# Head 0's operands from the pair's rows on chip, half the warm-up products, and the next pair's cluster products behind the transposes

## The chip, the cores and the metric

One core of a Trainium2 chip runs the whole program in one launch. The metric is device time in microseconds, of the kernel before and of the changed one on the same inputs; the median of several runs counts.

## The reference

Three layers follow each other on float32 data, with batch 2, 8 heads, 768 positions and head width 64.

```python
q_n, k_n, c_n = (x / (norm(x) + 1e-06) for x in (q, k, centroids))   # 16 centroids a head
q_assign = argmax(q_n @ c_n.T); k_assign = argmax(k_n @ c_n.T)
scores = where(q_assign[:, None] == k_assign[None, :], q @ k.T / 8, -1e9)
attn = softmax(scores) @ v
u = x + (relu(x.T @ w_tok1) @ w_tok2).T;   x = u + relu(u @ w_ch1) @ w_ch2
theta = x @ w_theta;  y = w_tok_r @ (x * cos(theta)) + w_tok_i @ (x * sin(theta))
out = (x + y) + relu((x + y) @ w_ch)
```

The change touches the first layer alone, the attention in which a query sees only the keys of its own cluster.

## The kernel before, in words

**Precision.** Every float32 operand is cut into a rounded high part and the remainder (`split_sb` for data in SBUF, `split_ps` for data in PSUM), so that products of parts add up to nearly full precision.

**Attention.** Heads come in pairs. `load_pair` loads the rows of a pair's q and k, 64 partitions a head, and `split_pair` cuts them on GpSimd. `masks` multiplies them with the centroids (the cluster products, tile `sim`, 4 products for the first pair and 12 for the others), turns them over on VectorE (`sT`), finds the largest of 16 (`mx`, `eq`, `eqT`), takes the first of equals by a triangular product (`pp`, `oh`) and writes the one-hot rows scaled (`m`). It is a generator that stops at each `yield`; the main loop takes two steps of it a unit. `place` copies 16 rows of `m` by DMA below the remainder rows in the tiles `q2` and `k2`, so that the second product of a score, `k2` by `q2`, adds the remainder and the mask at once. `prep` fills a head's four operand tiles by DMAs from the pair's parts; `prep_first`, used for heads 0 and 1, loads the head's rows from HBM instead, each twice, into both halves of a tile, and cuts them there.

A unit is 256 queries of a head. `scores` makes two tiles of 128 queries by 768 keys (4 products each, L354 and L355, into one of two PSUM buffers), takes the negated maximum (L359, `nm`) on VectorE and the exp (L361, `e`) on ScalarE. `turn` transposes the exp tiles on TensorE (L376) and cuts them, by ScalarE and VectorE (kind A) or by a ScalarE copy and two GpSimd operations (kind C, the third of each unit). `values` multiplies them with v (L399). Names end in batch, head, unit and tile: `s002` is the third score tile of head 0, `m02` the mask of pair 2.

**Order.** The program is written unit by unit; a scheduler then places each instruction on its engine's queue by its own timeline, in the order of writing where several are ready. `issue_after` keeps what is written inside it behind a named instruction. Engines and the DMA queue of SyncE (SP) work through their queues in order. SP issues nearly every load: rows of pairs, the copies of `prep` and `place`, and from unit 2 on, every four units, 512 columns of the weights w1 and w2 (`load_w`, L94 to L112), which ScalarE (L100, L101), VectorE (L103, L104) and GpSimd (L107) decode.

**Warm-ups.** `warm_up` issues products of a zero tile: `WARM` = 17 at the start, 4 behind the transposed centroids, 20 behind the first cluster products, 18 behind the first two score tiles.

**The start.** L475 loads pair 0's rows, L476 and L477 run its masks, L478 calls `prep_first` for head 0 and L480 for head 1; then `place` and `place_centroids` (clears `csth` and `cstl` on GpSimd, fills them on VectorE at L179). The upper halves of `q2` and `k2` are cleared on GpSimd at L205. In the first masks the rows go into head 0's tiles directly (L249 to L259).

The main loop, cut to the steps the change moves:

```python
for n in range(len(units) + SKEW):
    es[n] = scores(b, h, u, ops[b, h])
    for _ in range(PACE):
        next(gen, None)                     # masks of the next pair
    prs[n - 1] = turn(*units[n - 1], es.pop(n - 1))
    values(b, h, u, prs.pop(n - SKEW), ops[b, h][4])
```

Behind attention come two blocks of matrix products over all positions, which the change leaves as they are.

Of the kernel before, what the change touches and what calls it, by code (L numbers as in the profile page):

```python
# [9 lines left out]
F32 = mybir.dt.float32  # L10
# [8 lines left out]
P = 128  # L19
# [17 lines left out]
PACE = 2  # L37
# [7 lines left out]
SKEW = 2  # L45
WARM = (17, 4, 20, 18)


@with_exitstack
def tile_model(ctx: ExitStack, tc: tile.TileContext, qT, kT, v, cent, w1, w2, wc1, wc2, wth, wri, wch, out):  # L50
# [22 lines left out]
    def split_sb(h, l, x, rnd, sub):  # L73

        if rnd == "p":
            nc.gpsimd.tensor_scalar(out=h, in0=x, scalar1=1.0, scalar2=0.0, op0=ALU.mult, op1=ALU.add)
        elif rnd == "v":
            nc.vector.tensor_copy(out=h, in_=x)
        else:
            nc.scalar.activation(out=h, in_=x, func=AF.Copy)  # L80
        e = nc.gpsimd if sub == "p" else nc.vector
        e.tensor_tensor(out=l, in0=x, in1=h.bitcast(F32), op=ALU.subtract)

# [39 lines left out]
    with ExitStack() as actx:  # L123
# [45 lines left out]
        for j in range(2):  # L169
            r, n = slice(64 * j, 64 * j + 64), slice(96 + CL * j, 96 + CL * j + CL)  # L170
            nc.vector.tensor_copy(out=cst[r, n], in_=cps[r, CL * j : CL * j + CL])

# [31 lines left out]
        k2 = [ap.tile([P, S], F32R, name=f"k2_{i}") for i in range(2)]  # L204
        for t in q2 + k2:  # L205
            nc.gpsimd.memset(t[64:128, :].bitcast(F32), 0.0)

        def masks(b, pr):
# [27 lines left out]
            eqT = mp.tile([P, NH], BF16, tag="eq", bufs=2, name=f"eqT{b}{pr}")  # L236
            turned = nc.vector.transpose(out=eqT, in_=eq)
            marks.setdefault("eqT", turned)
            yield
# [5 lines left out]
            if first:  # L245
                for a in range(2):
                    n = slice(a * NH, a * NH + NH)
                    r = 32 * a
                    nc.vector.tensor_copy(out=q2[0][64 : 64 + CL, n], in_=oh[r : r + CL, :])  # L249
                    r = 64 + 32 * a  # L250
                    if a == 0:
                        nc.scalar.activation(  # L252
                            out=k2[0][64 : 64 + CL, n], in_=oh[r : r + CL, :], func=AF.Copy, scale=BIG, bias=-BIG
                        )
                    else:
                        nc.vector.tensor_scalar(
                            out=k2[0][64 : 64 + CL, n], in0=oh[r : r + CL, :], scalar1=BIG, scalar2=-BIG,
                            op0=ALU.mult, op1=ALU.add,
                        )  # L259
            yield  # L260
# [6 lines left out]
        def prep_first(b, h):  # L267
# [14 lines left out]
            nc.gpsimd.tensor_tensor(out=k1[64:128, :], in0=kr[64:128, :], in1=k1[64:128, :].bitcast(F32), op=ALU.subtract)  # L282
            return qh, q2[i], k1, k2[i], load_v(b, h)

        one = dict(scalar1=1.0, scalar2=0.0, op0=ALU.mult, op1=ALU.add)
# [18 lines left out]
        def split_pair(b, pr, ts):  # L304

            parts = []
            for x, f, k in zip(ts, (scale, 1.0), "qk"):
                hi, lo = (ap.tile([P, S], F32R, tag="hl", bufs=HL, name=f"{k}{j}{b}{pr}") for j in "hl")
                if f != 1.0:
                    nc.gpsimd.tensor_scalar(out=x, in0=x, scalar1=f, scalar2=0.0, op0=ALU.mult, op1=ALU.add)  # L310
                split_sb(hi, lo, x, "p", "p")
                parts += [hi, lo]
# [31 lines left out]
        def scores(b, h, u, ops):  # L344
# [3 lines left out]
            for j in range(2):  # L348
# [9 lines left out]
                nm = ap.tile([P, 1], F32, tag="nm", bufs=4, name=f"nm{b}{h}{qt}")  # L358
                nc.vector.tensor_reduce(out=nm, in_=ps[:, :, :NH], axis=AX.XY, op=ALU.max, negate=True)  # L359
                e = ap.tile([P, S], F32, tag="e", bufs=4, name=f"e{b}{h}{qt}")  # L360
# [7 lines left out]
        def turn(b, h, u, es):  # L368

            pr = []  # L370
            for j in range(NT // 2):
                ps = ps_t.tile([P, 2, 256], F32, tag="t", name=f"t{b}{h}{u}{j}")
                for i in range(2):
                    for a in range(2):
                        kt = 2 * j + a
                        nc.tensor.transpose(ps[:, a, i * P : i * P + P], es[i][:, kt * P : kt * P + P], ident)  # L376
                ph = ap.tile([P, 2, 256], F32R, tag="ph", bufs=6, name=f"ph{b}{h}{u}{j}")
                pl = ap.tile([P, 2, 256], F32R, tag="pl", bufs=6, name=f"pl{b}{h}{u}{j}")
                kind = KINDS[3 * u + j]
                if kind in "BC":  # L380
# [94 lines left out]
        raws = load_pair(0, 0)  # L475
        for _ in masks(0, 0):  # L476
            pass  # L477
        ops = {heads[0]: prep_first(*heads[0])}  # L478
        with tc.issue_after(marks["eqT"].ins):
            ops[heads[1]] = prep_first(*heads[1])  # L480
        place(1, ms[0, 0])
        place_centroids()
        gen = iter(())
# [4 lines left out]
        for n in range(len(units) + SKEW):  # L488
            if n < len(units):
# [4 lines left out]
                es[n] = scores(b, h, u, ops[b, h])  # L494
                if n == 0:
                    for w, k in zip(WARM[1:], ("cps", "sim", "scores")):
                        with tc.issue_after(marks[k].ins):
                            warm_up(w)
# [5 lines left out]
                if p1 < len(heads) // 2:  # L504
# [3 lines left out]
                    if n % 6 == PAIR_AT[1]:  # L508
                        split_pair(*pr, raws)
                    if n % 6 == PAIR_AT[2]:  # L510
                        gen = masks(*pr)
            for _ in range(PACE):
                next(gen, None)
            if n == 42:
                mctx.close()
            if 0 <= n - 1 < len(units):
                prs[n - 1] = turn(*units[n - 1], es.pop(n - 1))
            if 0 <= n - SKEW:
                b, h, u = units[n - SKEW]
# [257 lines left out]
```

## Time and profile before

| | |
|---|---|
| time, median of 3 runs | 690.68 us (689.6 to 693.99) |
| the profiled execution | 691.88 us, its span 690.2 us |
| mean granted TensorE clock | 0.988 |
| TensorE busy | 659.0 us, 95% |
| VectorE, ScalarE, GpSimd busy | 436.5, 372.8, 387.2 us |

The span runs from the first to the last instruction; the time holds the launch's ends too. A busy TensorE is one with products in its pipeline, at whichever clock. A clock of 1.00 is 2.4 GHz, 0.50 is 1.2 GHz. Idle time of an engine that nobody waits for costs nothing, so the chain of work that ended last and the idle times with their releasers say more than shares do.

### The profile page before, as it was taken

How to read it: one execution, taken by the hardware profiler on the slowest of the kernel's cores; microseconds unless marked ns; L12 is line 12 of the kernel's file. 1: busy time of each engine (PE TensorE's matmuls, PEld its weight loads, DVE VectorE, ACT ScalarE, POOL GpSimd, SP SyncE). 2: the span in 40 equal slices, each digit the busy share in tenths (PEclk: the TensorE clock that was granted, in tenths of full speed). 3: DMA queues.
4: the chain of work that ended last, by engine and by line, in shares of the span. 5: the costliest groups of instructions: out<-in, count | busy, mean ns of one | idle time of the engine just before them, and what ended most of it. 6: DMA issues, size and time to landing. Idle time of an engine off the chain costs nothing.

```text
span 690.2 us, 10585 instructions
## 1 busy us (share of the span) xinstructions
PE 659.0 (95%) x3772; PEld 578.1 (84%) x3772; DVE 436.5 (63%) x710; ACT 372.8 (54%) x722; POOL 387.2 (56%) x376
## 2 busy tenths in 40 slices
PE   7899989889999999999999999999999999999998
PEld 4798878788998999897888888888888777888886
DVE  6788788978888968558664533445657876523122
ACT  3687768676968777526553431135668684320000
POOL 8977779685866664437884640331456797432000
PEclk9899989999999999999999999999999999999999
DMA  9545645476344330003442321030021233320001
GB/s 264 142 108 165 173 106 146 104 222 180 81 93 92 86 76 1 1 1 123 134 142 92 122 91 33 9 114 2 0 62 61 88 95 93 123 61 32 16 30 47
DMA packets 24533, 62.27 MB, mean 90 GB/s; under 512 B 4320, under 2 KB 7584, under 8 KB 24480
## 3 DMA queue, kind: packets, MB, share of 16 engines
q1 hardware_dynamic: 24480, 61.59, 32.1%
q8 instruction: 30, 0.49, 0.3%
q14 instruction: 23, 0.19, 0.1%
HBM read 40.44 MB, written 3.15 MB: 63 GB/s over the span
## 4 chain that ended last, share of the span: by engine, by line
PE 74%; DVE 6%; DMA 6%; ACT 5%; POOL 4%; issue 3%; SPq 2%; ACTq 0%; POOLq 0%; DVEq 0%
PE o L399 7%; PE t L376 6%; PE r L118 5%; PE r L119 5%; PE r L120 5%; PE c L118 5%; PE c L119 5%; PE c L120 5%; PE y L120 4%; PE y L118 4%; PE y L119 4%; PE s L354 3%; PE s L355 3%; DMA w_raw<-w 3%; ACT e L361 2%
## 5 line engine op out<-in xcount | busy, mean ns | idle before, releaser
L359 DVE TENSOR_REDUCE nm<-s 128x1 f32<-128x768 f32 x96 | 90.9, 949 | 20.9 <-PE s L355 20.3
L361 ACT ACTIVATE e<-s,nm 128x768 f32<-128x768 f32 x96 | 86.9, 906 | 23.0 <-DVE nm L359 12.7
L376 PE MATMUL t<-ident,e 128*128 128x128 f32 x576 | 80.6, 275 | 5.9 <-DVE pl L86 4.7
L399 PE MATMUL o<-ph,vs 128*128 128x256 f32 x288 | 77.3, 298 | 3.0 <-DVE xt L406 3.0
L354 PE MATMUL s<-k,qh 128*128 128x384 f32 x192 | 70.7, 369 | 9.0 <-ACT e L361 6.8
L376 PEld LDWEIGHTS t<-ident,e 128*128 128x128 f32 x576 | 67.8, 142 | 10.5 <-DVE pl L86 4.3
L399 PE MATMUL o<-pl,vs 128*128 128x256 f32 x288 | 74.8, 291 | 0.3 <-POOL pl L387 0.3
L86 DVE TENSOR_TENSOR pl<-t,ph 128x512 fp32r<-128x512 f32 x96 | 62.9, 678 | 6.5 <-ACT ph L85 4.8
L355 PE MATMUL s<-k,q 128*128 128x384 f32 x192 | 65.7, 343 | 1.3 <-ACT k L252 1.3
L85 ACT ACTIVATE ph<-t 128x512 fp32r<-128x512 f32 x96 | 54.9, 598 | 17.6 <-PE t L376 14.8
L387 POOL TENSOR_TENSOR pl<-pr,ph 128x512 fp32r<-128x512 f32 x48 | 62.9, 1310 | 2.0
L386 POOL TENSOR_SCALAR ph<-pr 128x512 fp32r<-128x512 f32 x48 | 30.3, 632 | 57.6 <-ACT pr L382 51.4
L399 PEld LDWEIGHTS o<-ph,vs 128*128 128x128 f32 x288 | 56.1, 195 | 4.0 <-DVE xt L406 3.7
L118 PE MATMUL r<-ul,c_h 128*128 128x512 f32 x144 | 56.7, 394 | 0.0
L399 PEld LDWEIGHTS o<-pl,vs 128*128 128x128 f32 x288 | 56.1, 195 | 0.5 <-POOL pl L387 0.5
L118 PE MATMUL y<-zl,k_h 128*128 128x512 f32 x144 | 56.1, 390 | 0.0
L120 PE MATMUL y<-zh,k_h 128*128 128x512 f32 x144 | 56.1, 389 | 0.0
L119 PE MATMUL y<-zh,k_l 128*128 128x512 f32 x144 | 56.0, 389 | 0.0
L119 PE MATMUL r<-uh,c_l 128*128 128x512 f32 x144 | 56.0, 389 | 0.0
L120 PE MATMUL r<-uh,c_h 128*128 128x512 f32 x144 | 55.9, 389 | 0.0
L120 PE MATMUL c<-c_h,rh 128*128 128x512 f32 x144 | 55.9, 389 | 0.0
L119 PE MATMUL c<-c_h,rl 128*128 128x512 f32 x144 | 55.8, 389 | 0.0
(201 smaller groups left out, 1686.3 us busy)
## 6 DMA issues: line engine op xcount, KB each, us to landing
c_raw<-wc SPq DMA_DIRECT2D x24, 512.0 KB, 3.4
k_raw<-wri SPq DMA_DIRECT2D x18, 512.0 KB, 3.6
qh<-qh SPq DMA_DIRECT2D x28, 192.0 KB, 3.0
k<-kh SPq DMA_DIRECT2D x28, 192.0 KB, 3.7
ql<-qT SPq DMA_DIRECT2D x8, 384.0 KB, 4.2
kl<-kT SPq DMA_DIRECT2D x8, 384.0 KB, 4.4
vr<-v SPq DMA_DIRECT2D x16, 192.0 KB, 3.3
w_raw<-w SPq DMA_DIRECT2D x6, 512.0 KB, 4.0
```

The lines of the kernel that those rows point to most:

```text
L85: nc.scalar.activation(out=h, in_=ps, func=AF.Copy)
L86: nc.vector.tensor_tensor(out=l, in0=ps, in1=h.bitcast(F32), op=ALU.subtract)
L118: nc.tensor.matmul(ps, ah, bl, start=first and i == 0, stop=False)
L119: nc.tensor.matmul(ps, al, bh, start=False, stop=False)
L120: nc.tensor.matmul(ps, ah, bh, start=False, stop=last and i == n - 1)
L354: nc.tensor.matmul(ps[:, half, :NH], qh[:, c], k1[:, n], start=True, stop=False)
L355: last = nc.tensor.matmul(ps[:, half, :NH], ql[:, c], kk[:, n], start=False, stop=True)
L359: nc.vector.tensor_reduce(out=nm, in_=ps[:, :, :NH], axis=AX.XY, op=ALU.max, negate=True)
L361: nc.scalar.activation(out=e.rearrange("p (a n) -> p a n", a=2), in_=ps[:, :, :NH], func=AF.Exp, bias=nm, accum_out=sums[b, h // 2][:, qt, ...
L376: nc.tensor.transpose(ps[:, a, i * P : i * P + P], es[i][:, kt * P : kt * P + P], ident)
L387: nc.gpsimd.tensor_tensor(out=pl, in0=raw, in1=ph.bitcast(F32), op=ALU.subtract)
L399: nc.tensor.matmul(ps[:, :256], vs[:, kt, :], p[:, kt % 2, :], start=n == 0 and k == 0, stop=n == NT - 1 and k == 1,)
```

## The change

Head 0's four operand tiles are made from the pair's rows, which are on chip for the cluster products anyway (`prep_pair_first`): two ScalarE operations, one GpSimd and two VectorE operations, and one more on ScalarE, each of 64 partitions. The subtraction of k, on GpSimd before, is VectorE's. The clears of `q2` and `k2` are split, head 1's behind the copy of k. Head 1's `prep_first` is issued behind the first unit's maxima. The scaled k rows of the first mask are both ScalarE's. The third tiles of units 0 and 1 of head 0 are cut by ScalarE and VectorE in place of GpSimd. The next pair's mask steps are written behind `turn` in place of ahead of it, and for three units are kept behind a transpose. The cutting of later pairs is kept behind the one before. The fourth group of warm-ups has 9 products.

```diff
-WARM = (17, 4, 20, 18)
+WARM = (17, 4, 20, 9)
...
-        for t in q2 + k2:
-            nc.gpsimd.memset(t[64:128, :].bitcast(F32), 0.0)
+        def clear(i):
+            for t in (q2[i], k2[i]):
+                nc.gpsimd.memset(t[64:128, :].bitcast(F32), 0.0)
+        clear(0)
...
-                    if a == 0:
-                        nc.scalar.activation(
-                            out=k2[0][64 : 64 + CL, n], in_=oh[r : r + CL, :], func=AF.Copy, scale=BIG, bias=-BIG
-                        )
-                    else:
-                        nc.vector.tensor_scalar(
...
+                    nc.scalar.activation(
+                        out=k2[0][64 : 64 + CL, n], in_=oh[r : r + CL, :], func=AF.Copy, scale=BIG, bias=-BIG
+                    )
...
+        def prep_pair_first(ts):
+            q, k = (t[0:64, :] for t in ts)
+            qh = ap.tile([P, S], F32R, tag="qh", bufs=2, name="qh00")
+            k1 = ap.tile([P, S], F32R, tag="k1", bufs=2, name="k100")
+            marks["k1"] = nc.gpsimd.tensor_scalar(out=k1[0:64, :], in0=k, **one)
+            nc.scalar.activation(out=qh[0:64, :], in_=q, func=AF.Copy, scale=scale)
+            nc.vector.tensor_tensor(out=k1[64:128, :], in0=k, in1=k1[0:64, :].bitcast(F32), op=ALU.subtract)
+            nc.scalar.activation(out=qh[64:128, :], in_=q, func=AF.Copy, scale=scale)
+            nc.vector.scalar_tensor_tensor(
+                out=q2[0][0:64, :], in0=q, scalar=scale, in1=qh[0:64, :].bitcast(F32), op0=ALU.mult, op1=ALU.subtract
+            )
+            nc.scalar.activation(out=k2[0][0:64, :], in_=k, func=AF.Copy)
+            return qh, q2[0], k1, k2[0]
...
-                kind = KINDS[3 * u + j]
+                kind = "A" if (b, h) == (0, 0) and u < 2 else KINDS[3 * u + j]
...
-        for _ in masks(0, 0):
+        first = masks(0, 0)
+        next(first)
+        vs00 = load_v(0, 0)
+        with tc.issue_after(marks["cst"].ins):
+            ops = {heads[0]: prep_pair_first(raws) + (vs00,)}
+        for _ in first:
             pass
-        ops = {heads[0]: prep_first(*heads[0])}
-        with tc.issue_after(marks["eqT"].ins):
-            ops[heads[1]] = prep_first(*heads[1])
+        with tc.issue_after(marks["k1"].ins):
+            clear(1)
+            place_centroids()
         place(1, ms[0, 0])
-        place_centroids()
...
                 if n == 0:
+                    with tc.issue_after(marks["max"].ins):
+                        ops[heads[1]] = prep_first(*heads[1])
...
-                        split_pair(*pr, raws)
+                        with tc.issue_after(marks["cut"].ins) if p1 > 1 else nullcontext():
+                            split_pair(*pr, raws)
...
-            for _ in range(PACE):
-                next(gen, None)
             if n == 42:
                 mctx.close()
             if 0 <= n - 1 < len(units):
                 prs[n - 1] = turn(*units[n - 1], es.pop(n - 1))
+            with tc.issue_after((marks["turn"] if n else marks["scores"]).ins) if n < 3 else nullcontext():
+                for _ in range(PACE):
+                    next(gen, None)
```

At the start VectorE's queue stands so before, from the centroids' copy to the end of the first cluster search. `cst`, `csth` and `cstl` are placed centroids, `q_0` is head 0's `q2`:

```order
L171 COPY cst<-cps 64x16 x2
L86 TENSOR_TENSOR ctl<-cps,cth 128x128
L179 CAST csth<-cth 64x4x16 x2
L179 CAST cstl<-ctl 64x4x16 x2
L279 SCALAR_TENSOR_TENSOR q_0_155<-qr_190,qh_196 64x768
L224 STREAM_TRANSPOSE sT_172<-sim_167 128x384
```

And so in the changed kernel:

```order
L171 COPY cst<-cps 64x16 x2
L291 SCALAR_TENSOR_TENSOR q_0_155<-ql_161,qh_177 64x768
L289 TENSOR_TENSOR k_178<-kl_163,k_178 64x768
L86 TENSOR_TENSOR ctl<-cps,cth 128x128
L179 CAST csth<-cth 64x4x16 x2
L228 STREAM_TRANSPOSE sT_170<-sim_165 128x384
L179 CAST cstl<-ctl 64x4x16 x2
```

Head 0's two remainders have come ahead of the placed centroids, and `sT` between the two pairs of casts.

On the same engine around units 10 and 11, where pair 2's mask `m02` is written, before (`nm` maxima, `pl` remainders of exp tiles, `xt` output rows):

```order
L244 SCALAR_TENSOR_TENSOR oh02_957<-pp02_958,eqT02_875 128x384
L406 TENSOR_TENSOR xt02_669<-o020_906,tmp020_919 64x256
L359 TENSOR_REDUCE nm032_1013<-s032_1008 128x1
L86 TENSOR_TENSOR pl0220_969<-t0220_963,ph0220_968 128x512
L262 TENSOR_SCALAR m02_961<-oh02_957,mab_150 128x384
L86 TENSOR_TENSOR pl0221_978<-t0221_972,ph0221_977 128x512
L359 TENSOR_REDUCE nm033_1022<-s033_1017 128x1
```

And in the changed kernel:

```order
L418 TENSOR_TENSOR xt02_651<-o020_888,tmp020_901 64x256
L371 TENSOR_REDUCE nm032_995<-s032_990 128x1
L86 TENSOR_TENSOR pl0220_945<-t0220_939,ph0220_944 128x512
L371 TENSOR_REDUCE nm033_1004<-s033_999 128x1
L86 TENSOR_TENSOR pl0221_954<-t0221_948,ph0221_953 128x512
L247 SCALAR_TENSOR_TENSOR oh02_968<-pp02_969,eqT02_886 128x384
L371 TENSOR_REDUCE nm034_1087<-s034_1082 128x1
L259 TENSOR_SCALAR m02_972<-oh02_968,mab_150 128x384
```

`m02` has moved behind `nm033`, `pl0221` and `nm034`.

SP's queue around the placing of that mask, before, and the load of the weights `w1_2`:

```order
L290 DMA vr05_1195<-v 128x384
L322 DMA q2_0_155<-m02_961 16x384 x2
L322 DMA k2_0_157<-m02_961 16x384 x2
L94 DMA w1_2_raw_1088<-w1 128x1024
L322 DMA q2_1_156<-m02_961 16x384
```

And in the changed kernel:

```order
L302 DMA vr05_1177<-v 128x384
L349 DMA qh05_1165<-qh02_691 64x768
L334 DMA q2_0_155<-m02_972 16x384 x2
L334 DMA k2_0_157<-m02_972 16x384 x2
L94 DMA w1_2_raw_1070<-w1 128x1024
```

A load of `qh05` has come ahead of the placing.

## Rows read from the trace of the kernel before

**Rows 1.** Busy time by stretch (us, busy us of each engine, granted clock, DMA share, GB/s).

```profile
14.30:21.20 6.90, 6.02 (x25) 4.50 (x26) 4.65 (x7) 3.68 (x6) 6.74 (x8) 0.51 0.56 190
30.00:40.00 10.00, 9.53 (x70) 8.80 (x71) 9.89 (x17) 8.86 (x20) 7.31 (x7) 1.00 0.58 135
...
89.50:96.40 6.90, 5.77 (x24) 5.70 (x25) 5.24 (x9) 2.97 (x6) 4.18 (x4) 0.51 0.88 182
```

**Rows 2.** Chain of work that ended last, first 60 us (start us, us, what).

```profile
4.16 5.17 DMA kr<-kT
...
10.99 2.09 POOL k L282
...
13.74 0.19 PE pp L243
...
13.96 0.57 DVE oh L244
...
17.50 3.86 PE wps L140 x18
21.36 0.17 PE s L354
```

**Rows 3.** Timeline of ScalarE, start (start us, us, what, [idle before <-releaser]).

```profile
18.23 0.90 ACT L361 ACTIVATE e<-s,nm 128x768 f32<-128x768 f32 x1 [1.80 <-DVE nm L359]
```

**Rows 4.** Tile kl, first load, issued at 1.80 us.

```profile
DMA to landing us min/median/max: 4.5/4.5/4.5
```

**Rows 5.** Timeline of VectorE, start.

```profile
5.76 0.36 DVE L171 COPY cst<-cps 64x16 f32<-64x16 f32 x2 [0.48 <-PE cps L162]
...
6.73 0.49 DVE L179 CAST csth<-cth 64x64 fp32r<-64x64 f32 x2
...
8.79 0.95 DVE L279 SCALAR_TENSOR_TENSOR q<-qr,qh 64x768 fp32r<-64x768 f32 x1 [1.16 <-ACT qh L276]
9.66 0.57 DVE L224 STREAM_TRANSPOSE sT<-sim 128x384 f32<-128x384 f32 x1
...
11.44 0.58 DVE L237 STREAM_TRANSPOSE eqT<-eq 128x384 bf16<-128x384 bf16 x1
...
25.23 0.96 DVE L359 TENSOR_REDUCE nm<-s 128x1 f32<-128x768 f32 x1 [1.30 <-PE s L355]
```

**Rows 6.** Timeline of GpSimd, start.

```profile
1.91 0.73 POOL L206 MEMSET q<- 64x768 f32 x1
...
5.25 0.85 POOL L176 MEMSET csth<- 128x896 f32 x1
...
9.50 0.93 POOL L277 TENSOR_SCALAR k<-kr 128x768 fp32r<-128x768 f32 x1 [2.32 <-DMA kr<-kT]
...
17.20 1.80 POOL L282 TENSOR_TENSOR k<-kr,k 64x768 fp32r<-64x768 f32 x1
```

**Rows 7.** Timeline of VectorE, 117 to 127 us.

```profile
123.08 1.68 DVE L104 SCALAR_TENSOR_TENSOR w_f<-w_f,w_raw 128x512 uint32<-128x512 uint32 x1
```

**Rows 8.** Timeline of GpSimd, the same stretch.

```profile
122.96 1.26 POOL L387 TENSOR_TENSOR pl<-pr,ph 128x512 fp32r<-128x512 f32 x1
```

**Rows 9.** Timeline of VectorE, around m02.

```profile
69.18 0.67 DVE L86 TENSOR_TENSOR pl<-t,ph 128x512 fp32r<-128x512 f32 x1
69.78 0.94 DVE L359 TENSOR_REDUCE nm<-s 128x1 f32<-128x768 f32 x1
```

**Rows 10.** Timeline of SP's queue, around m02's placing.

```profile
69.28 1.18 SPq L322 DMA_DIRECT2D q<-m  x2
...
80.70 0.64 SPq L94 DMA_DIRECT2D w_raw<-w  x1
```

**Rows 11.** Timeline of ScalarE, 52 to 88 us.

```profile
54.12 0.67 ACT L100 ACTIVATE w_f<-w_raw 128x512 f32<-128x512 f32 x1 [1.24 <-DMA w_raw<-w]
...
78.37 0.60 ACT L382 ACTIVATE pr<-t 128x512 f32<-128x512 f32 x1
```

**Rows 12.** Who waited for whom, 30 to 315 us (us in total, times, longest).

```profile
ACT w_f L100 <- DMA w_raw<-w: 5.9, 5, 2.1
```

More of the change, by code (lines that the diff above doesn't have):

```diff
@@ L1 @@
 import math
-from contextlib import ExitStack
+from contextlib import ExitStack, nullcontext
 import concourse.bass as bass
@@ L81, in split_sb @@
         e = nc.gpsimd if sub == "p" else nc.vector
-        e.tensor_tensor(out=l, in0=x, in1=h.bitcast(F32), op=ALU.subtract)
+        return e.tensor_tensor(out=l, in0=x, in1=h.bitcast(F32), op=ALU.subtract)
     def split_ps(h, l, ps):
@@ L170, in tile_model @@
             r, n = slice(64 * j, 64 * j + 64), slice(96 + CL * j, 96 + CL * j + CL)
-            nc.vector.tensor_copy(out=cst[r, n], in_=cps[r, CL * j : CL * j + CL])
+            marks["cst"] = nc.vector.tensor_copy(out=cst[r, n], in_=cps[r, CL * j : CL * j + CL])
         def place_centroids():
@@ L236, in masks @@
             eqT = mp.tile([P, NH], BF16, tag="eq", bufs=2, name=f"eqT{b}{pr}")
-            turned = nc.vector.transpose(out=eqT, in_=eq)
-            marks.setdefault("eqT", turned)
+            nc.vector.transpose(out=eqT, in_=eq)
             yield
@@ L250, in masks @@
                     r = 64 + 32 * a
-                    if a == 0:
-                        nc.scalar.activation(
-                            out=k2[0][64 : 64 + CL, n], in_=oh[r : r + CL, :], func=AF.Copy, scale=BIG, bias=-BIG
-                        )
-                    else:
-                        nc.vector.tensor_scalar(
-                            out=k2[0][64 : 64 + CL, n], in0=oh[r : r + CL, :], scalar1=BIG, scalar2=-BIG,
-                            op0=ALU.mult, op1=ALU.add,
-                        )
+                    nc.scalar.activation(
+                        out=k2[0][64 : 64 + CL, n], in_=oh[r : r + CL, :], func=AF.Copy, scale=BIG, bias=-BIG
+                    )
             yield
@@ L310, in split_pair @@
                     nc.gpsimd.tensor_scalar(out=x, in0=x, scalar1=f, scalar2=0.0, op0=ALU.mult, op1=ALU.add)
-                split_sb(hi, lo, x, "p", "p")
+                marks["cut"] = split_sb(hi, lo, x, "p", "p")
                 parts += [hi, lo]
@@ L358, in scores @@
                 nm = ap.tile([P, 1], F32, tag="nm", bufs=4, name=f"nm{b}{h}{qt}")
-                nc.vector.tensor_reduce(out=nm, in_=ps[:, :, :NH], axis=AX.XY, op=ALU.max, negate=True)
+                marks["max"] = nc.vector.tensor_reduce(out=nm, in_=ps[:, :, :NH], axis=AX.XY, op=ALU.max, negate=True)
                 e = ap.tile([P, S], F32, tag="e", bufs=4, name=f"e{b}{h}{qt}")
@@ L375, in turn @@
                         kt = 2 * j + a
-                        nc.tensor.transpose(ps[:, a, i * P : i * P + P], es[i][:, kt * P : kt * P + P], ident)
+                        marks["turn"] = nc.tensor.transpose(ps[:, a, i * P : i * P + P], es[i][:, kt * P : kt * P + P], ident)
                 ph = ap.tile([P, 2, 256], F32R, tag="ph", bufs=6, name=f"ph{b}{h}{u}{j}")
                 pl = ap.tile([P, 2, 256], F32R, tag="pl", bufs=6, name=f"pl{b}{h}{u}{j}")
-                kind = KINDS[3 * u + j]
+                kind = "A" if (b, h) == (0, 0) and u < 2 else KINDS[3 * u + j]
                 if kind in "BC":
```

## Prediction, made without a run of the changed kernel

> **What bounds the kernel now.** I read busy time by stretch, the chain of work that ended last, each engine's timeline over the first 26 us, and then who waits for whom in the middle of attention. Between 30 and 40 us TensorE is busy 9.53 of 10 us [rows 1], and the page's slices show nine tenths or more behind attention, which ends near 311 us. What can be won lies in the first 25 us and in the stalls of attention.
>
> At the start the chain is a line of waits [rows 2]. The second copy of head 0's k from HBM is issued at 4.16 and takes 5.17 us; GpSimd rounds it and subtracts until 13.08; TensorE has stood at that wait and gives pp late; VectorE makes oh from 13.96, and the products that lacked its rows end at 17.50. Then 18 warm-up products hold TensorE until 21.36, though the exp that frees a score buffer ended at 18.23 + 0.90 = 19.13 [rows 3]. So a load, a GpSimd subtraction and warm-ups longer than what they cover stand in a row.
>
> The granted clock from 14.3 to 21.2 us is 0.51 [rows 1], the lower of the two levels, 1.2 GHz; TensorE had stood idle ahead of it, at the wait for k. A warm-up costs 3.86/18 = 0.214 us there.
>
> **The change part by part.** The sum is made against the profiled execution's own 691.88 us (span 690.2 and 1.7 around it). The median of the runs shown is 690.68, 1.2 lower, and the gain is taken off that.
>
> *Operands of head 0 from the pair's rows.* Four loads and head 0's own copies go. What is late next? The pair's k rows land at 1.80 + 4.5 = 6.3 [rows 4]; q, issued ahead of it, feeds ScalarE, which has nothing to do then. VectorE, free at 5.76 + 0.36 = 6.12, makes the q remainder until 7.07 (0.95) [rows 5]. GpSimd copies k in 0.93 [rows 6]; as this lies beside a two-input operation of VectorE I add 0.29, by which the subtraction L282 was longer at 10.99 (2.09) [rows 2], where VectorE ran such operations too, than at 17.20 (1.80) [rows 6]: until 7.5. The subtraction of k on VectorE has no row: it lies between the 0.95 of the q remainder and GpSimd's 2.09. I take 1.0, next to the row that has its engine and size. It ends at 8.5, not 13.08.
>
> Most of that is lost again, because VectorE's order changes too: the casts into csth now stand ahead of sT, and they wait for GpSimd's clearing of csth, which comes behind the copy of k and two other clears: 7.5 + 2 x 0.73 + 0.85 = 9.8 [rows 6]. With 0.49 for the casts sT starts at 10.3. Before, sT to the end of eqT took 9.66 to 12.02, 2.36 us [rows 5]; the casts into cstl now stand in between (0.49 at most): 13.15, against 12.02. But pp then follows at once, since TensorE no longer stands at k, and the clears and casts are done. From pp's start to oh's 0.22 us passed (13.74 to 13.96 [rows 2]); with as much as 0.35, for pp's own start too, oh starts at 13.5, not 13.96: **0.46 us**.
>
> The collision can be harder than 0.29. L104 on VectorE took 1.68 from 123.08, beside a GpSimd subtraction that ran from 122.96 to 124.22 [rows 7, 8]: it ended 0.5 us after that one, as if it had first waited it out. Then the copy of k would start at 7.07 and end at 8.0, and the 0.46 is gone. The Trainium skill's page "SBUF — State Buffer" (section "The single rule") says that of a VectorE instruction with two SBUF inputs and a GpSimd instruction that reads SBUF the second one blocks until the first is done. By it the sum would be 0.5 smaller; the row of 123.08 agrees, the 0.29 of L282 is too little for it.
>
> *A second block of mask rows goes from VectorE to ScalarE.* One operation each way, beside TensorE's first products. I count nothing; without that cover it is one operation of about half a microsecond.
>
> *Nine warm-ups less.* 9 x 0.214 = **1.93 us** [rows 2]. The products end at 17.50 - 0.46 = 17.04, nine warm-ups at 18.97. The exp before s002 starts at 18.23 - 0.46 = 17.77 and ends at 18.67 [rows 3], so the warm-ups still end last, by 0.3 us.
>
> Sum for s002: 2.39 us earlier. But it runs at the low clock: its first product at 21.36 shows 0.17 [rows 2], at half clock 0.34, four of them cost 0.7 more. **1.7 us** is left. Bounds: 0.5 less with the harder collision; if the clock did not fall this time, the six products before (6 x 0.17) would end 1.0 earlier too and the exp would decide, s002 at 17.7, 3.7 gained.
>
> *Work moved between engines.* Two tiles of exp values leave GpSimd for VectorE, 2 x 0.67 = 1.34 us [rows 9]. VectorE is busy 9.89 of 10 us from 30 to 40 [rows 1], so this isn't free; its cover is the wait of 1.30 before the row at 25.23 [rows 5], which goes as the scores now follow closely. Head 1's q remainder moves behind the first two maxima, into VectorE's next wait for scores. Cost taken 0, up to 1.3 if that cover fails.
>
> *Cluster products behind the transposes.* The order is rearranged through all of attention. In pair 2, m02 now stands behind nm033, pl0221 and nm034: 0.94 + 0.67 + 0.94 = 2.55 us later [rows 9]. SP issues in order: the placing of m02 from 69.28, then the weights w1_2 [rows 10]. A load of qh05 (an issue is 0.6 [rows 10]) stands ahead of both now: 3.1 later. ScalarE reaches w1_2 later by e035 and two copies, 0.90 + 2 x 0.60 = 2.1 [rows 3, 11], so its wait there grows by **1.0**. w2_0 was issued at 80.70, 14 issues behind 69.28, 0.82 each; now 15, from a start 2.55 later: 3.35, against 2.2 on ScalarE (three copies and a shorter one): **1.15** more. w1_1, however, is issued where it was, behind s015, and ScalarE reaches it behind e023 and three copies, 2.7 later: the wait of **1.24** [rows 11] goes. Together +0.9 on ScalarE, of which TensorE sees a part. All w loads cost ScalarE 5.9 us in 5 waits [rows 12]. From below: these all go. From above: the masks of the next two pairs are later alike, +3.3 in all. I take 0, next to the sum of the three.
>
> Forecast: 690.68 - 1.7 = **689.0 us**, its own range 685.5 to 692.
>
> **The rivals.**
>
> *A, slower: the late masks.* w1_2, w2_0 and the two w2 loads behind them wait longer by about 1 us each (3.3 in all with w1_1's gain), all of it reaches TensorE, and one more stretch falls to half clock as 89.5 to 96.4 did (6.9 us at 0.51 [rows 1], 3.4 us lost): 689.0 + 6.7 = 695.7. It decides as soon as these weights land over 2 us after ScalarE reaches them. For it: 5 of the 6 loads already come late. Against it: the same order puts transposes and value products between the halves of s040, which gives placing time.
>
> *B, much faster: the new order loses the stalls.* Half of the 5.9 us reaches TensorE (2.9) and goes, and the half-clock stretch with it (3.4): 689.0 - 6.3 = 682.7. For it: w1_1, and transposes that start right behind s002. Against it: w1_2 and w2_0.
>
> *C, the clock stays low at the start.* Before, warm-ups filled most of the low stretch; now real work does. If the clock comes back one such stretch later, 6.9 us at half speed cost 3.4: 692.4. Against it: from s002 on TensorE has scores, transposes and cluster products in a row.
>
> *D, the start gives the warm-ups only.* With the copy of k blocked the 0.46 goes: 689.5. It is the case where the change doesn't do what it says, the clears being late where k was.
>
> **How the numbers follow.** Forecast 0.43, B 0.20, A 0.14, D 0.12, C 0.11. About 1%, 6.9 us, is what a measurement of this kernel can tell from no change (three runs before span 689.6 to 693.99). Faster by more means below 683.8: most of B, 0.16, and 0.02 of the forecast's tail. Slower means above 697.6: nearly half of A, 0.06, and 0.01 of C. The rest is 0.75. The range goes from B's time to A's, 682.7 to 695.7; the outer halves of both are left out.
>
> **What would show it.** Right: the csth casts wait for GpSimd and sT starts near 10.3; oh near 13.5; nine warm-ups end near 19; in the middle no wait before w1_1's L100, and some 2 us before w1_2's and w2_0's. D: oh at 13.9 or later. C: a clock of 0.5 granted beyond 22 us. A or B: ScalarE's waits for w loads well above or below 5.9 us, and more or fewer half-clock stretches behind 80 us. I am wrong if s002 comes less than 1 us earlier, or if the time moves by over 6 us.

## The result and the profile after

The changed kernel takes 698.21 us (median of 9 runs, 694.02 to 699.14), the kernel before 691.15 beside it (9 runs, 689.6 to 693.99). The ratio is 1.0086, its 95% interval 1.0061 to 1.0111: about 6 us slower. The prediction was 689.0, its range 682.7 to 695.7.

The profiled execution took 699.14 us, span 697.4, against 691.88 and 690.2. It is the longest of the nine runs. The granted clock of these two executions is as low on the mean, 0.987 against 0.988, so the 7 us between them are not the clock's. From the page, the span and the busy time of the engines after:

```profile
span 697.4 us, 10544 instructions
...
PE 659.6 (95%) x3763; PEld 576.8 (83%) x3763; DVE 442.7 (63%) x712; ACT 374.4 (54%) x724; POOL 382.8 (55%) x371
```

TensorE stands idle for 697.4 - 659.6 = 37.8 us; before it was 690.2 - 659.0 = 31.2. Nearly all of the loss is idle time of TensorE, and it does not arise at the start: the maxima of head 0 come 0.3 us earlier to 1.5 later than before, those of head 6 come 1.0 to 3.3 earlier, those of head 9 come 3.7 to 6.8 later. Head 6's lead is not the new start's merit: by then the kernel before has had its stretch of half clock from 89.5 to 96.4 [rows 1], and the changed kernel's comes only at 133.8. The same view as [rows 12], who waited for whom from 30 to 315 us (us in total, times, longest), after:

```profile
PE s L366 <- ACT e L373: 10.7, 12, 2.0
...
ACT w_f L100 <- DMA w_raw<-w: 8.7, 4, 3.6
...
PE o L411 <- DVE xt L418: 6.0, 6, 2.6
...
ACT c_raw L101 <- DMA c_raw<-wc: 2.3, 1, 2.3
...
ACT c_f L100 <- DMA c_raw<-wc: 1.6, 1, 1.6
```

And of the kernel before, beside the row of [rows 12]:

```profile
PE s L354 <- ACT e L361: 5.5, 7, 1.7
PE t L376 <- DVE pl L86: 4.7, 5, 2.4
PE o L399 <- DVE xt L406: 3.0, 2, 2.6
...
ACT c_raw L101 <- DMA c_raw<-wc: 2.2, 1, 2.2
```

ScalarE waits 12.6 us for loads instead of 8.1; TensorE's wait for transposed tiles' remainders (`pl`) shrinks, but its waits for the exp and for the output rows `xt` double. The timelines show one behind the other. ScalarE's timeline after, the weight casts that answer to [rows 11]:

```profile
56.48 0.69 ACT L100 ACTIVATE w_f<-w_raw 128x512 f32<-128x512 f32 x1 [0.99 <-DMA w_raw<-w]
...
81.43 0.65 ACT L100 ACTIVATE w_f<-w_raw 128x512 f32<-128x512 f32 x1 [3.65 <-DMA w_raw<-w]
...
151.99 0.66 ACT L100 ACTIVATE w_f<-w_raw 128x512 f32<-128x512 f32 x1 [2.34 <-DMA w_raw<-w]
...
161.26 0.67 ACT L100 ACTIVATE c_f<-c_raw 128x512 f32<-128x512 f32 x1 [1.61 <-DMA c_raw<-wc]
```

and TensorE's timeline right behind three of them:

```profile
83.69 0.39 PE L411 MATMUL o<-ph,vs 128*128 128x256 f32 x1 [2.56 <-DVE xt L418]
...
154.15 0.45 PE L366 MATMUL s<-k,qh 128*128 128x384 f32 x1 [2.03 <-ACT e L373]
...
164.40 0.44 PE L366 MATMUL s<-k,qh 128*128 128x384 f32 x1 [1.67 <-ACT e L373]
```

Behind each wait of ScalarE for a load (3.65, 2.34, 1.61) a stall of TensorE of much the same length (2.56, 2.03, 1.67) ends 2 to 3 us later. The loads stand on SP behind the placing of mask rows, and the masks are late already at 40 us. That this lateness is what costs the time is not shown; e1 and e4 below speak against it. Start of the masks m01 to m10 on VectorE, and of the issue of the loads w1_1, w1_2, w2_0 and w2_2 on SP (us):

```
               m01   m02    m03    m10  |  w1_1  w1_2  w2_0   w2_2
before        37.4  68.4  103.5  136.3  |  50.2  71.8  80.7  139.3
changed       40.8  72.4  105.9  142.6  |  52.7  76.4  84.9  146.3
```

At the start of the changed kernel the chain of work that ended last (start, us, what) reads, beside [rows 2]:

```profile
1.81 4.29 DMA kl<-kT
6.18 1.42 POOL k L287
...
9.11 0.86 POOL csth L176
...
10.80 0.46 DVE csth L179
11.29 0.58 DVE sT L228
...
14.53 0.49 PE pp L246
15.04 0.57 DVE oh L247
...
15.69 0.52 ACT k L254
...
16.24 0.53 ACT k L254
...
16.80 0.66 PE s L367
```

and in the kernel before, behind `oh` at 13.96 [rows 2]:

```profile
14.61 0.53 ACT k L252
...
15.18 0.69 PE s L355
```

The second load of k is gone, but GpSimd's clear of `csth` and the casts stand in its place, and `oh` starts at 15.04, not 13.96.

### The profile page after: what moved, and what is told of

It is laid out like the page before. It is cut to its first block, busy times and chain, and to the rows that moved or that the text cites. A ratio compares the mean times of both kernels' runs of the same rounds, so it can differ in the third digit from the quotient of the medians.

```text
span 697.4 us, 10544 instructions
## 1 busy us (share of the span) xinstructions
PE 659.6 (95%) x3763; PEld 576.8 (83%) x3763; DVE 442.7 (63%) x712; ACT 374.4 (54%) x724; POOL 382.8 (55%) x371
## 3 DMA queue, kind: packets, MB, share of 16 engines
q1 hardware_dynamic: 24160, 60.80, 31.2%
## 4 chain that ended last, share of the span: by engine, by line
PE 74%; DVE 7%; ACT 5%; POOL 5%; DMA 5%; issue 3%; SPq 1%; ACTq 0%; POOLq 0%
PE o L411 8%; PE t L388 6%; PE r L118 5%; PE r L120 5%; PE r L119 5%; PE c L118 5%; PE c L119 5%; PE c L120 5%; PE y L119 4%; PE y L120 4%; PE y L118 4%; PE s L366 3%; PE s L367 3%; PE po L118 2%; PE po L120 2%
## 5 line engine op out<-in xcount | busy, mean ns | idle before, releaser
L86 DVE TENSOR_TENSOR pl<-t,ph 128x512 fp32r<-128x512 f32 x98 | 64.7, 679 | 6.0 <-ACT ph L85 5.5
L398 POOL TENSOR_SCALAR ph<-pr 128x512 fp32r<-128x512 f32 x46 | 28.8, 626 | 61.2 <-ACT pr L394 52.5
L399 POOL TENSOR_TENSOR pl<-pr,ph 128x512 fp32r<-128x512 f32 x46 | 60.3, 1312 | 1.8
```

Source lines behind the costliest of these rows:

```text
L86: nc.vector.tensor_tensor(out=l, in0=ps, in1=h.bitcast(F32), op=ALU.subtract)
L399: nc.gpsimd.tensor_tensor(out=pl, in0=raw, in1=ph.bitcast(F32), op=ALU.subtract)
```

## The experiments

Ratios are to the kernel before on the same chip, with 95% intervals. The chips differ, so microseconds of different runs are compared by their ratios, taken times 690. "Start" is the new start (operands from the pair's rows, clears, second mask block on ScalarE, two tiles off GpSimd, 9 warm-ups), "steps" the mask steps behind the transposes, "rule" the rule that keeps the cutting of a pair behind the one before.

```
after  start + steps + rule                          1.0086  [1.0061, 1.0111]
e1     start + rule                                  1.0098  [1.0067, 1.0128]
e2     steps                                         0.9966  [0.9953, 0.9980]
e3     after, csth/cstl casts behind the mask        1.0089  [1.0067, 1.0112]
e4     start                                         1.0000  [0.9969, 1.0032]
e5     start + steps                                 1.0066  [1.0043, 1.0088]
e6     rule                                          1.0017  [1.0001, 1.0033]
e7     9 warm-ups                                    0.9988  [0.9971, 1.0006]
e8     start + steps, casts on ScalarE               1.0021  [0.9999, 1.0044]
e9     after, early loads                            1.0047  [1.0025, 1.0068]
e10    steps, early loads                            0.9987  [0.9969, 1.0005]
e11    before, early loads                           0.9975  [0.9957, 0.9992]
e12    e8, early loads (the first weights too)       1.0004  [0.9989, 1.0019]
e13    after, two tiles on GpSimd again              0.9997  [0.9980, 1.0014]
e14    e8, two tiles on GpSimd again                 0.9954  [0.9936, 0.9972]
e15    steps + 9 warm-ups                            0.9973  [0.9956, 0.9990]
e16    steps + rule                                  1.0013  [1.0000, 1.0026]
e17    two tiles off GpSimd                          1.0040  [1.0024, 1.0057]
e18    e14, early loads                              0.9956  [0.9938, 0.9974]
```

### Which of the parts: e1, e2, e4, e5, e6, e16

The first theory (M) was that the steps behind the transposes made the masks late. e1 puts them back ahead of `turn`, e2 makes that one edit in the kernel before:

```diff
-            for _ in range(PACE):
-                next(gen, None)
...
                 prs[n - 1] = turn(*units[n - 1], es.pop(n - 1))
+            with tc.issue_after((marks["turn"] if n else marks["scores"]).ins) if n < 3 else nullcontext():
+                for _ in range(PACE):
+                    next(gen, None)
```

> The changed kernel with the mask steps of the next pair written ahead of the transposes again, all else as changed. Theory M (late masks: the 6 to 7 us come from the mask steps behind the transposes, by way of late placing, late weights on SP and ScalarE waiting for them): back to the kernel before or a little under it, 690 to 692 us; ScalarE's waits for w loads at L100 near 5.9 us again instead of 10.3. Theory S (the loss is the start's: csth ahead of sT, slow q casts): stays at 697 to 699. Theory R (any new order is good for a few us either way, through TensorE stalls and half-clock stretches, whatever the masks do): somewhere from 690 to 699 with the L100 waits unrelated to it.

> The kernel before with that one edit alone: the mask steps written behind the transposes, kept behind a transpose for three units. Theory M: 696 to 699 us, L100 waits of 9 to 11 us. Theory S: 690 to 692. Theory R: anything from 688 to 699.

Measured: 696.45 us (1.0098) and 687.39 us (0.9966). Theory M falls on both: without the steps the loss stays, and alone they make the kernel 2.3 us faster. In e1's profile (its shortest run, 692.85 us) ScalarE's waits for loads are back at 6.4 us, as M had said,

```profile
ACT w_f L100 <- DMA w_raw<-w: 5.7, 5, 1.8
...
ACT c_raw L101 <- DMA c_raw<-wc: 0.7, 1, 0.7
```

and this run too is 3.2 us over the median of the kernel before beside it (689.69): the waits and the time do not go together. e4 leaves the start alone, e1 without the rule:

```diff
-                        with tc.issue_after(marks["cut"].ins) if p1 > 1 else nullcontext():
-                            split_pair(*pr, raws)
+                        split_pair(*pr, raws)
```

> The changed kernel with the mask steps ahead of the transposes and without the cutting of later pairs kept behind the one before: what is left is the new start (pair operands, clears, second mask block on ScalarE, two tiles off GpSimd, 9 warm-ups). Theory M: s002 0.2 to 0.5 us earlier than in the kernel before, 690 to 692 us. Theory S: 697 to 699. Theory R: differs from e1 by 2 us or more although only the cutting differs.

Measured: 689.88 us (1.0000). e1 and e4 differ by 0.0098 and in the rule alone, the sign named for theory R. The masks and loads of e4 are nearly as late as the changed kernel's and cost nothing; those of e1 come about as early as before:

```
               m01   m02    m03    m10  |  w1_1  w1_2  w2_0   w2_2
e1            36.7  69.2  103.5  137.2  |  48.8  72.2  80.9  140.2
e4            40.4  72.1  105.1  137.3  |  52.5  75.1  84.8  140.3
```

So next the rule was suspected (K): e5 takes only it out of the changed kernel, e6 puts only it into the kernel before.

> The changed kernel without the rule that keeps the cutting of later pairs behind the one before, all else as changed (mask steps behind the transposes). Theory K (the loss of 6 us is this rule's: it moves GpSimd's scalings and cuts, and TensorE's cluster products and ScalarE's weight casts come out later): 687 to 691 us, TensorE's idle time 3 to 6 us less than the 37.8 of the changed kernel. Theory M (late masks): stays at 696 to 699. Theory R (any new order moves the time by a few us): 690 to 698.

> The kernel before with that rule alone. Theory K: 693 to 698 us. Theory M: 689 to 691. Theory R: anything from 686 to 697.

Measured: 692.22 (1.0066) and 690.01 us (1.0017). The rule costs about 1 us alone, hardly told from none; K falls as the whole. Each part alone costs next to nothing, yet the start together with either of the others costs 4 to 7 us. The last pair is steps and rule without the start:

> The kernel before with the mask steps moved and the rule on the cutting, but with its old start. If the parts simply add: 0.9966 times 1.0017, 687 to 689 us. If the rule and the steps together are what costs (masks late by both): 692 us or more. If the loss needs the new start: 686 to 689.

Measured: 690.45 us (1.0013), between the ranges that were named, 0.003 over the two together (0.9983) and far from 1.0086. The loss needs the start. What one edit is worth depends on what stands beside it: the steps are a gain of 2.3 us alone and a loss of 4.6 us on top of the start (e4 to e5), the rule costs 1.2 us alone and 6.8 us on top of the start (e4 to e1). Theory R, by which any new order moves the time by a few us, is not ruled out by these runs.

### The start's own gain: e3, e7, e8

e3 keeps the casts into `csth` and `cstl` behind the first mask, with a mark on m00 and the casts in a block behind it:

```diff
+            marks.setdefault("m", made)
...
-            place_centroids()
+            cut_centroids()
+        with tc.issue_after(marks["m"].ins):
+            place_centroids()
```

> The changed kernel with VectorE's casts into csth and cstl kept behind the first mask m00 (GpSimd's clears stay where they are). Theory M: the start gets faster and the middle keeps its loss: sT at 8.9 instead of 11.3, oh near 12.6 instead of 15.0, s002 near 18.6 instead of 20.8, the time 2 us under the changed kernel, 695 to 697. Theory S: 4 to 7 us under it, 691 to 694. Theory R: the start as by M, the time anywhere within 5 us of the changed kernel.

Measured: 695.95 us (1.0089). `sT` started at 8.45 and `oh` at 11.24, but s002 only at 20.00. VectorE's timeline of e3 shows where the 3.8 us went:

```profile
14.23 2.00 DVE L182 CAST csth<-cth 64x64 fp32r<-64x64 f32 x2
16.24 1.69 DVE L182 CAST cstl<-ctl 64x64 fp32r<-64x64 f32 x2
17.96 1.82 DVE L375 TENSOR_REDUCE nm<-s 128x1 f32<-128x768 f32 x2
```

and GpSimd's beside it:

```profile
14.18 1.80 POOL L283 TENSOR_TENSOR k<-kr,k 64x768 fp32r<-64x768 f32 x1
16.05 1.03 POOL L82 TENSOR_TENSOR vs<-vr,vs 128x384 fp32r<-128x384 f32 x1
17.05 0.83 POOL L76 TENSOR_SCALAR qh<-ql 128x768 fp32r<-128x768 f32 x1
```

In the kernel before two such casts take 0.39, with GpSimd idle from 7.18 on; the 0.49 of [rows 5] still lies beside the end of a clear:

```profile
7.24 0.39 DVE L179 CAST cstl<-ctl 64x64 fp32r<-64x64 f32 x2
```

In e3 the first two begin 0.05 behind a GpSimd subtraction and end 0.25 behind its end; the maxima stand behind all four. e7 is the kernel before with `WARM = (17, 4, 20, 9)`; e8 is e5 with these casts on ScalarE, which waits there:

```diff
-                    nc.vector.tensor_copy(
+                    nc.scalar.activation(
...
+                        func=AF.Copy,
```

> The kernel before with 9 warm-up products in the fourth group in place of 18 and nothing else. The prediction's term: s002 1.9 us earlier, 1.2 to 1.9 us of it left at the end, 688 to 689. The rival (what the start gains, the heads behind it give back, since loads and GpSimd's work there set when they go on): within 1 us of before.

> The kernel of e5 with the casts into csth and cstl on ScalarE, which stands idle there, in place of VectorE. sT near 8.5 and oh near 11.3 as in e3, the first maxima near 13.5 to 14 in place of 18, s002 near 15.5 to 17 in place of 20. If the start's gain reaches the end: 3 to 4 us below e5. If the heads behind it give it back: within 1 us of e5.

Measured: 687.77 us (0.9988), a gain of 0.8 us that is not told apart from none; and 689.28 us (1.0021), 3 us under e5, as was said for a gain that reaches the end, and still not under the kernel before. In e8 s002 starts at 16.62 and the maxima of head 0 come up to 4.5 us before those of the kernel before, but in heads 5 to 7 they stand within 0.2 us of those of e2, which has the old start. VectorE's timeline of e8 shows one place where the lead shrinks:

```profile
26.43 0.58 DVE L229 STREAM_TRANSPOSE sT<-sim 128x384 f32<-128x384 f32 x1 [2.49 <-PE sim L120]
```

and GpSimd's what that waited for, the cut of the next pair's k:

```profile
22.82 2.19 POOL L82 TENSOR_TENSOR kl<-kl,kh 128x768 fp32r<-128x768 f32 x1
```

It is not the whole of it: in e14, which has the two tiles back on GpSimd, `sT` starts no sooner (26.28), and heads 5 to 7 still come 3.6 us before those of e8.

### The late loads: e9 to e12

Theory W: what the parts cost together is ScalarE's waiting for late weights. A load is kept behind the operands of the head before the last, in place of behind the last placing, so that it is issued some 20 us sooner, and ScalarE's casts of it are kept behind the exps:

```diff
-                with tc.issue_after(placed[0].ins):
+                with tc.issue_after((moves[-2] if len(moves) > 1 else placed[0]).ins), tc.issue_after(marks["exp"].ins):
```

> The changed kernel with each load of weights kept behind the operands of the head before the last instead of behind the last placing of mask rows, so that it is issued some 20 us sooner, and its casts on ScalarE kept behind the exps of their unit. Theory W (what the three parts cost together is ScalarE's waiting for late weights: 14.6 us of waits in the changed kernel's profile against 8.1 before): those waits fall under 4 us, TensorE's idle time from 37.8 to about 31, the time to 690 to 693 us. Theory R (the sum of many small stalls, whatever the loads do): the waits go and the time stays at 695 to 699.

> The kernel before with the same earlier loads and nothing else. Theory W: the 8.1 us of waits go and 3 to 5 us with them, 684 to 686 us. Theory R: 687 to 692.

Measured: 691.59 us (1.0047) and 686.94 us (0.9975). Who waited for whom on ScalarE in e9, 30 to 315 us:

```profile
ACT c_raw L101 <- DMA c_raw<-wc: 2.9, 2, 2.7
```

No wait for `w_raw` is left (the changed kernel's waits for loads add up to 13.2 us with one at 25 us, not the 14.6 of the expectation), TensorE's idle time is 686.7 - 656.0 = 30.7 in its profile, which is of its shortest run, and 2.7 us of the 6 come back, plus or minus 2.3. So the earlier loads, with the casts behind the exps, win back a part of the loss, not all of it. For the kernel before (e11) the time is between the two ranges that were named.

> The kernel of e2 (the mask steps alone moved) with the same earlier loads. Theory W: 3 to 5 us under e2, 682 to 685 us. Theory R: 686 to 690.

> The kernel of e8 (no rule on the cutting, casts into csth and cstl on ScalarE) with the earlier loads, the first weights too, which are issued behind the first values. Theory W: oh near 11.3, s002 near 16 to 17, and no wait of ScalarE at 25 us, so that the start's gain stays: 680 to 685 us. Theory R: 687 to 692.

Measured: 687.83 (0.9987) and 688.86 us (1.0004). Theory W's numbers were not reached, and e10 is no faster than e2, though its waits for loads on ScalarE fall from 7.6 us to 3.1.

### The two tiles: e13, e14, e17

VectorE after, from 23.20 to 41 us, has only two waits, of 0.19 and 0.24 us. Busy time from 23 to 41 us (us, busy us of TensorE, its weight loads, VectorE, ScalarE and GpSimd, granted clock, DMA share, GB/s), before:

```profile
23.00:41.00 18.00, 16.21 (x114) 15.18 (x115) 16.24 (x26) 14.71 (x30) 13.17 (x13) 1.00 0.50 125
```

after:

```profile
23.00:41.00 18.00, 16.89 (x118) 15.39 (x117) 17.20 (x27) 15.04 (x31) 6.78 (x7) 1.00 0.52 146
```

GpSimd has lost half of its work there, VectorE is at 17.20 of 18. In GpSimd's timeline after, the first tile that it still cuts comes behind a long wait:

```profile
37.55 0.62 POOL L398 TENSOR_SCALAR ph<-pr 128x512 fp32r<-128x512 f32 x1 [6.58 <-ACT pr L394]
```

Theory V: the two tiles moved there are what makes the masks late. e13 takes only them back:

```diff
-                kind = "A" if (b, h) == (0, 0) and u < 2 else KINDS[3 * u + j]
+                kind = KINDS[3 * u + j]
```

> The changed kernel with the two tiles of head 0 cut on GpSimd as before, all else as changed. Theory V (VectorE has no gap from 23 to 41 us in the changed kernel while GpSimd stands idle for 6.6 us, so the 1.35 us of the two tiles, priced at nothing in the prediction, delay the masks and with them the loads): m01 at 38 to 39.5 us in place of 40.8, the weights w1_1 issued 1 to 2 us sooner, the time 1.5 to 4 us under the changed kernel, 694 to 697. Theory W alone (late loads, from whatever cause behind 60 us): within 1 us of the changed kernel, 697 to 699.

Measured: 689.18 us (0.9997): the whole loss is gone, more than theory V had said. e13's profile is of its shortest run (687.05 us, mean clock 0.994), the changed kernel's of its longest (699.14 us, 0.987), so the two are further apart than the ratios are. The same stretch in e13:

```profile
23.00:41.00 18.00, 17.46 (x127) 16.71 (x126) 16.30 (x27) 14.85 (x32) 12.42 (x14) 1.00 0.50 132
```

VectorE has 1.7 us of room, TensorE is busy 0.57 us more. But e1, which has the two tiles on VectorE and loses as much as the changed kernel, has the same room:

```profile
23.00:41.00 18.00, 16.13 (x115) 14.62 (x114) 16.33 (x27) 13.98 (x30) 5.71 (x6) 1.00 0.49 130
```

So the edit is what costs the time in the changed kernel; that it does so by filling VectorE before 41 us, as theory V has it, is not shown. In e13's profile masks and loads come sooner than in the changed kernel throughout (here beside e17's), and ScalarE's waits for loads fall to 7.7 us:

```
               m01   m02    m03    m10  |  w1_1  w1_2  w2_0   w2_2
e13           36.5  69.6  102.2  134.9  |  47.6  72.6  81.1  137.9
e17           37.7  71.4  104.9  138.2  |  49.9  74.3  83.0  141.3
```

```profile
ACT w_f L100 <- DMA w_raw<-w: 4.7, 4, 1.8
ACT c_raw L101 <- DMA c_raw<-wc: 2.3, 1, 2.3
...
ACT c_f L100 <- DMA c_raw<-wc: 0.7, 1, 0.7
```

> The kernel of e8 with the two tiles on GpSimd again. Theory V: VectorE has room from 26 to 38 us and the 4 us that e8 wins in head 0 last beyond head 3: 685 to 687. The rival (in e8 the transposed similarities wait 2.5 us for GpSimd's cut of k, which ends at 25 us whatever VectorE does): m01 stays near 39, 688 to 690.

> The kernel before with only the two tiles of head 0 cut by ScalarE and VectorE in place of GpSimd. Theory V in its strong form (the two tiles by themselves cost the 6 us): 693 to 696. Theory V in its weak form (they cost where VectorE is short of time, and in the kernel before, whose head 0 starts as late but whose VectorE has a gap of 1.3 us at 25 us, there is room): 689 to 692, m01 1 to 2 us later than 37.4.

Measured: e14 687.07 us (0.9954), the best of all with e18, with m01 at 36.4, so the rival falls; e17 691.68 us (1.0040, 2.8 us). In e17 m01 is hardly later, but m02 is by 3.0 us and w1_2 by 2.5. So the two tiles cost 2.8 us alone, within the range of V's weak form, 4.6 us in e8 (e14 to e8), and 6.1 us (0.0089 of 690, plus or minus 2) inside the change. Of the edits tried more than once this is the one that costs clearly each time.

### Combinations: e15, e18

> The kernel of e2 (mask steps behind the transposes) with 9 warm-ups and nothing else: the two parts that did not cost anything by themselves. If they add: 0.9966 times 0.9988 of the kernel before, 685.5 to 687 us. If not (the order behind the warm-ups changes with them): 687 to 690.

> The kernel of e14 (casts into csth and cstl on ScalarE, no rule on the cutting, two tiles on GpSimd) with the earlier loads of e9. If late loads still cost it anything (3.07 us of wait at 75 us, 1.92 and 2.16 us at 152 to 161 us): 684 to 686 us, under e14's 687.1. If the loads no longer set the end: 686.5 to 688.5.

Measured: 687.01 (0.9973) and 685.79 us (0.9956). The warm-ups add nothing to e2. e18's 685.79 lies in the range named for loads that still cost, but its ratio, 0.9956 against e14's 0.9954, does not tell a gain of the earlier loads from none. The start and the steps of the change, without the rule, with GpSimd's two tiles left and the casts on ScalarE, beat both kernels: 3 us under the one before.

## Why the prediction was wrong

*The step that failed* is "Two tiles of exp values leave GpSimd for VectorE ... Cost taken 0, up to 1.3". The section saw that VectorE is busy 9.89 of 10 us from 30 to 40 [rows 1] and still took one wait of 1.30 at 25.23 [rows 5] as cover for it and for head 1's q remainder. In the changed kernel that wait is not there: the remainder took 1.39 from 20.51, not 0.95, and VectorE ran on to 41 us. And the bound of 1.3, the tiles' own length, was no bound: the two tiles measured 2.8 us alone and 6.1 in the change, where taking them back takes the whole loss away (e13). In the changed kernel's profile the mask is late, and behind it the placing, the load and ScalarE; but e4 is late by as much and loses nothing, and e1 is not late and loses as much. By which path the two tiles cost it stays open.

*Operands of head 0.* The pair's k was there at 6.18 (6.3 said), the copy on GpSimd ended at 7.59 (7.5), the subtraction on VectorE took 0.95 (1.0), the clear of `csth` ended at 9.96 (9.8). Two casts into `csth` then took 1.27, not 0.49, the first of them beside the clear of `cstl`, and `oh` came at 15.04, not 13.5: 1.1 us lost where 0.46 were to be won. In e13, with the same start, GpSimd's copy began before the q remainder, `sT` started at 10.12 and `oh` at 13.71, near the forecast. Which of the two comes first changes from profile to profile, as the load lands a little sooner or later.

Here the collision has its rows. VectorE and GpSimd in the changed kernel:

```profile
5.94 0.95 DVE L291 SCALAR_TENSOR_TENSOR q<-ql,qh 64x768 fp32r<-64x768 f32 x1 [0.16 <-ACT qh L288]
```

```profile
6.18 1.41 POOL L287 TENSOR_SCALAR k<-kl 64x768 fp32r<-64x768 f32 x1 [1.92 <-DMA kl<-kT]
```

and in e4, where GpSimd began first:

```profile
5.95 1.33 DVE L291 SCALAR_TENSOR_TENSOR q<-ql,qh 64x768 fp32r<-64x768 f32 x1
```

```profile
5.65 0.82 POOL L287 TENSOR_SCALAR k<-kl 64x768 fp32r<-64x768 f32 x1 [1.40 <-DMA kl<-kT]
```

The first one keeps its own length (0.95, 0.82), the second ends 0.70 and 0.81 us behind the first one's end, nearly as if it had only begun there. The Trainium skill's page "SBUF — State Buffer" (section "SBUF: two separate sides") says that of a VectorE operation with two SBUF inputs and a GpSimd operation that reads SBUF, whichever starts first has the pair of ports that they share for the whole instruction, and the other fully blocks; the trace agrees to within some 0.1 us. The 0.29 taken from L282 was too little.

*The second block of mask rows* was counted as nothing, or half a microsecond without its cover. The cover was not there: from `oh` to the first product that waits for these rows 1.76 us pass (15.04 to 16.80), with two ScalarE operations in a row, where it was 1.22 (13.96 to 15.18), with one.

*Nine warm-ups less.* They ended at 21.0, not 18.97, as `oh` was late, and s002 came 0.2 us earlier, not 2.39 (TensorE, before and after; the chain's 21.36 in [rows 2] counts from the end of the warm-ups, which is 21.0 now):

```profile
21.02 0.52 PE L354 MATMUL s<-k,qh 128*128 128x384 f32 x1
```

```profile
20.81 0.47 PE L366 MATMUL s<-k,qh 128*128 128x384 f32 x1
```

That is the sign named as wrong, "s002 comes less than 1 us earlier". Alone (e7) the term was worth 0.8 us at the end, not told apart from none. In e13's profile, where `oh` came at 13.71, s002 started at 19.63, 1.4 us earlier, and the time is still that of the kernel before.

*Cluster products behind the transposes*, taken as 0 between -5.9 and +3.3, were worth -2.3 alone (e2), but +4.6 on top of the start (e4 to e5). Two of the three waits went the way that was said: in e2 w1_1's fell from 1.24 to 0.31 and w1_2's grew to 2.67 (about 2 said); w2_0's went, where 2.3 had been said. In the changed kernel w1_1's was 0.99 and w1_2's 3.65.

*The rule on the cutting* had no term in the prediction at all. It cost 1.2 us alone (e6), and 6.8 on top of the start (e4 to e1).

*The rivals.* A named the right sign and the waits that the changed kernel's profile shows, late masks and late weights on SP, and 695.7 is 2.5 us under what came. That is luck in part: it gave the cause to the steps, and without them the loss stays (e1); the waits do not carry it in e1 either; and its further stretch of half clock did not come: the stretches of the changed kernel, by the same view as [rows 1], are

```profile
133.80:140.60 6.80, 6.24 (x30) 6.24 (x31) 3.44 (x8) 2.12 (x4) 0.00 (x0) 0.52 0.00 0
577.50:580.90 3.40, 3.40 (x10) 2.59 (x10) 2.97 (x4) 1.12 (x2) 3.40 (x4) 0.53 0.52 159
14.30:21.10 6.80, 4.78 (x17) 3.31 (x17) 5.99 (x8) 3.66 (x6) 6.55 (x6) 0.52 0.13 36
```

where the kernel before has those at 14.3 and 89.5 [rows 1] and one of 3.4 us at 147: as much low clock, elsewhere. C did not come (the clock was back at 21.1). D, the start that gives the warm-ups only, is nearest to what the start did, and even of these only 0.2 us was left at s002; it is not what set the time. B's lost stalls came in part: the waits for `pl` fell from 4.7 to 1.0.

Open stays why the two tiles cost 2.8 us alone and 6.1 in the change. That the new start leaves VectorE no room behind 20 us does not explain it: e1's profile has the new start and as much room as e13's. The clock may be a part: e17's runs have a mean granted clock of 0.995 where the kernel before beside them has 0.991, the changed kernel's nine have 0.988 where e13's have 0.9925. The start without the two tiles and without the other parts was not run. The parts of this change do not add: e2, e6, e7 and e17 sum to +0.9 us.

## What to carry to other kernels

An operation given to an engine that shows no gap in a stretch is not free, and its own length is no bound for what it costs. Before an expensive wait is blamed on the edit that sits beside it, take single edits back, from the whole change and alone: here the suspected one was a gain alone and a loss beside the new start. A chain of waits in one profile is a suspicion: look for a kernel that has the waits without the loss, or the loss without the waits (here e4 and e1). And a faster start can be gone some heads later: e8 leads e2 by up to 4.0 us in head 0 and by nothing in heads 5 to 7.

## What the runs showed of the hardware

Two casts of 64x64 on VectorE, 0.39 us with GpSimd idle, took 1.27 beside a GpSimd clear and the rounding behind it, the first of the two ending at 10.80 and the clear at 10.74, and 2.00 and 1.69 beside GpSimd subtractions and a rounding (e3): these casts are held by a GpSimd operation that is already running. Not every VectorE operation is: the transposition `eqT` took 0.58 at 13.89 in the changed kernel, beside a GpSimd scaling, and 0.56 at 32.77, with GpSimd idle.

The runs of one kernel differ by more than was expected: the changed kernel's nine go from 694.0 to 699.1 us, at mean clocks of 0.993 down to 0.982, so that one profile of each does not tell 6 us apart; the intervals do. And the clock has a part in the ratios. Of the 138 runs of the kernel before beside the experiments, the 36 with the lowest mean clock (0.988 and less) take 690.0 us on the mean and the 36 with the highest (0.994 and more) 687.4. The kernels that beat it (e2, e11, e14, e15, e18) have 0.994 to 0.997 on the mean of their runs where it has 0.989 to 0.991 beside them, so what they would gain at the same clock is not shown; e17 and e6 lose at a clock that is higher than its.
